# Turning x of eleven late chunks by DMA transposes on the SP queue instead of TensorE and ScalarE

## The chip, the cores and the metric

The kernel runs on one core of a Trainium2 chip. The metric is the device time of one execution in microseconds (us), the median of several runs. A core has four compute engines (TensorE, VectorE, ScalarE, GpSimd), a sequencer SP that here issues nearly all DMAs, and sixteen DMA engines that carry them. In the profile's lines PE is TensorE, PEld its weight loads, DVE VectorE, ACT ScalarE, POOL GpSimd; SPq is SP's sequencer.

## The reference

A gated linear attention with state runs over 768 positions for 4 batches and 8 heads of 48; its output, taken as x of 384 columns, goes through a gated MLP with a spatial mix.

```
state = alpha[t] * state + k[t] (outer) v[t];   y[t] = q[t] @ state        # 4 batches x 8 heads, head_dim 48
x = y as [4, 768, 384]
h = relu(x @ w_in);  u, v = halves of h (512 each)
v_n = (v - mean) / sqrt(var + 1e-6);  v_s = w_spatial @ v_n + b_spatial
out = (u * v_s) @ w_out
```

## The kernel before

The sequence is cut into 24 chunks of 128 positions, 6 per batch. Each chunk loads alpha, k, q, v (192 KB each, called ac, kc, qc, vc), computes y in PSUM and hands x to the second half, which needs it transposed as xT: the v matmuls of the same chunk, and the u matmuls of three chunks, read xT.

The order of all instructions is not written by hand. A small planner in the kernel gives each operation an estimated duration, plays all of them against each other with hints (NUDGE, PATIENCE), and emits each engine's program in the order that comes out. The planner's times are only used for that; on the chip the engines wait on semaphores. SP's program is part of the order, and in the traces below SP issues its DMAs in the order of its program.

```python
    def dma(key, us, emit, deps, prio, eng="SP", issue=0.99, lat=1.9):
        o = op(key + ("issue",), eng, issue, emit, deps, prio=prio)          # time of the issuing sequencer
        return op(key, "DMA", us, lambda _: None, [o], prio=prio, lat=lat)   # time of the DMA engines, then latency
...
        op(("xs", i), "ACT", 0.38, xs, ...)          # x_sb <- y: PSUM to SBUF, bf16
        def xt(_):                                   # three 128x128 transposes on TensorE, into y's PSUM bank
            for ks in range(KS):
                nc.tensor.transpose(xv[:, ks, :], st["x_sb"][:, ks, :], ident)
        op(("xt", i), "PE", 0.2, xt, got(("xs", i)), ...)
        op(("xe", i), ENGINES["xe"], None, xe, ...)  # xT <- PSUM, on ScalarE
...
        dma(("ac", i), LD, load("ac", alpha), io_users("ln", j), P, lat=LATE)      # kc, qc, vc likewise
...
        group(("v", b, tt), mms, 0.22, got(("xe", b * NCH + tt)) + made[("w_in", 1)], Q + tt, evac, ...)
```

Of the kernel before, what the change touches and what calls it, by code (L numbers as in the profile page):

```python
# [9 lines left out]
FP32 = mybir.dt.float32  # L10
# [41 lines left out]
class Clock:  # L52
# [34 lines left out]
NUDGE = {  # L87
    ("m", 9, 0): -0.15,
    ("vn", 0, 4): -0.3,
    ("qt", 22): -0.3,  # L90
    ("upd", 2): 0.3,
    ("v", 0, 5): 0.6,
    ("vbp", 0, 0): -0.6,
    ("z", 21): 1.5,
    ("ebc", 0): 0.15,
    ("ev", "q", 1, 1): 0.15,
    ("z", 19): -1.5,
    ("cast", "w_in", 0, 1): -0.15,
    ("vb", 21): -0.15,
    ("y", 19): -1.5,  # L100
    ("kc", 0): 1,
# [4 lines left out]
    ("y", 2): 0.15,  # L106
    ("xs", 22): -0.3,
    ("m", 20, 0): 0.6,
}
PAIRS = (0, 1, 2)  # L110
LATE = 3.5
ACT_STATS = ((2, 2), (0, 2))
PIECES = {
    "w_in": ((0, "vc", 1, 0.35), (0, "kc", 2, 0.15)),
    "w_sp": ((0, "vc", 4, 0.35), (0, "qc", 6, 0.25), (0, "qc", 6, 0.25)),
    "w_out": (0, "qc", 7, 0.25),
}

# [46 lines left out]
def kernel(  # L165
# [12 lines left out]
    nc = tc.nc  # L178

    B, H, S, D = q.shape  # L180
    C = 128
    NCH = S // C
    HP = H // 2
    DM = H * D
# [13 lines left out]
    WK = 3  # L198
# [3 lines left out]
    raws = ctx.enter_context(tc.tile_pool(name="raws", bufs=NRAW))  # L202
# [28 lines left out]
    def copy(eng, out, in_):  # L231
        if eng == "ACT":
            nc.scalar.copy(out=out, in_=in_)  # L233
        else:
            ENG[eng].tensor_copy(out=out, in_=in_)  # L235
# [79 lines left out]
    made = {}  # L315

    def op(key, *args, **kw):

        users = kw.pop("use", ())
        o = Op(*args, **kw)  # L320
        for s in users:
            s.users.append(o)
        ops.append(o)
        made[key] = o
        o.wait = PATIENCE.get(key[0], 0.0) + NUDGE.get(key, 0.0)
        return o

    def got(*keys):
        return [made.get(x) for x in keys]

    def dma(key, us, emit, deps, prio, eng="SP", issue=0.99, lat=1.9):
        o = op(key + ("issue",), eng, issue, emit, deps, prio=prio)
        return op(key, "DMA", us, lambda _: None, [o], prio=prio, lat=lat)
# [38 lines left out]
    def finish_x(i):  # L372

        b, c = divmod(i, NCH)
        t0 = c * C
        st = T[i]
        P = float(10 * i)

        def xs(eng):
            st["x_sb"] = work.tile([128, KS, 128], BF16, name="x_sb")  # L380
            copy(eng, st["x_sb"], st["y"].rearrange("p h d -> p (h d)").rearrange("p (k t) -> p k t", k=KS))

        op(("xs", i), "ACT", 0.38, xs, got(("y", i), ("xt", i - WK)), prio=P + 9, use=[st["sl_y"]])

        def xt(_):
            xv = st["xv"] = st["y"].rearrange("p h d -> p (h d)").bitcast(BF16)[:, 0:KS * 128].rearrange(
                "p (ks t) -> p ks t", ks=KS)
            for ks in range(KS):
                nc.tensor.transpose(xv[:, ks, :], st["x_sb"][:, ks, :], ident)  # L389

        op(("xt", i), "PE", 0.2, xt, got(("xs", i)), prio=P + 9, use=[st["sl_y"]], cols=384)

        def xe(eng):
            if c == 0:
                tiles(b)
            to, fr = bt[b]["xT"][:, :, t0:t0 + C], st["xv"]
            if i // 2 in PAIRS:
                to = to.rearrange("p k (t two) -> p k t two", two=2)
                fr = fr.rearrange("p k (two t) -> p k t two", two=2)
            copy(eng, to, fr)  # L400

        op(("xe", i), ENGINES["xe"], None, xe,
           got(("xt", i)) + [made.get(("all", b - 3))], prio=P + 9, use=[st["sl_y"]])

    def io_users(x, j, back=None):

        j = j - IO if back is None else j
        if x == "cum":
            return got(("cum", 2 * j), ("cum", 2 * j + 1), ("cump", j, 0), ("cump", j, 1))
        return got((x, 2 * j), (x, 2 * j + 1), (x + "p", j), (x + "p", j, 0), (x + "p", j, 1))  # L410
# [5 lines left out]
    def pair(j):  # L416
# [172 lines left out]
        for ci in range(2):  # L589
            i = 2 * j + ci  # L590
            T[i]["sl_y"] = Slot(rings["a"])

            def y(_, i=i, ci=ci):
                yt = T[i]["y"] = bank(pp_a, [128, H, D], FP32, name="y", tag="a")
                rows = halves(ci)
                n, tot = 0, 2 * H + (HP if i % NCH else 0)
                for h in range(H):
                    for par in range(2):
                        nc.tensor.matmul(  # L599
                            out=yt[:, h, :], lhsT=st[f"ptm{par}"][rows, h % 2, h // 2, :],  # L600
                            rhs=st["vb"][rows, par, h, :], start=(n == 0), stop=(n == tot - 1))
                        n += 1
                if i % NCH:
                    for hp in range(HP):
                        nc.tensor.matmul(
                            out=yt[:, 2 * hp:2 * hp + 2, :].rearrange("p s d -> p (s d)"),
                            lhsT=q_cols(slice(0, 128), hp, ci), rhs=sbd_bufs[(i - 1) % NB][:, hp, :],
                            start=False, stop=(n == tot - 1))
                        n += 1

            op(("y", i), "PE", 0.5, y,
               [made[("m", j, par, s)] for par in range(2) for s in range(2)]
               + got(("vbp", j, 0), ("vbp", j, 1)) + (got(("sb", i - 1)) if i % NCH else []), prio=P + 8 + ci, take=T[i]["sl_y"], cols=1024)
            finish_x(i)

    def first(i):
# [6 lines left out]
        def load(name, src):  # L623
            def emit(_):
                if i % 2 == 0:
                    T[i + 1][name + "2"] = st[name + "2"] = io_pool.tile([128, 2, H, D], FP32, name=name)
                t = st[name] = st[name + "2"][:, i % 2]
                nc.sync.dma_start(out=t, in_=src[b, :, t0:t0 + C, :].rearrange("h s d -> s h d"))
            return emit

        j = i // 2
        jo = j - NKP
        dma(("ac", i), LD, load("ac", alpha), io_users("ln", j), P, lat=LATE)
        dma(("kc", i), LD, load("kc", k), io_users("kt", j), P + 0.1, lat=LATE)
        dma(("qc", i), LD, load("qc", q), io_users("qt", j), P + 0.2, lat=LATE)
        dma(("vc", i), LD, load("vc", v), io_users("vb", j), P + 0.3, lat=LATE)

# [107 lines left out]
        def y(_):  # L745
# [16 lines left out]
        op(("y", i), "PE", 0.38 if c else 0.2, y, got(("m", i, 0), ("m", i, 1), ("vb", i), ("sb", i - 1) if c else None),  # L762
           prio=P + 8, take=st["sl_y"], cols=768)
        finish_x(i)


    bt = {}

    def tiles(b):
        d = bt[b] = {}  # L770
        d["xT"] = batch.tile([128, KS, S], BF16, name="xT")
        d["uT"] = batch.tile([128, NDS, S], BF16, name="uT")
        d["v_sb"] = batch.tile([128, NT, DH], BF16, name="v_sb", bufs=2)
        d["vn"] = batch.tile([128, NT, DH], BF16, name="vn", bufs=2)
        d["gT"] = batch.tile([128, NDS, S], BF16, name="gT", bufs=2)
        d["mvs"] = batch.tile([128, NT, 2], FP32, name="mvs")
        d["sums"] = batch.tile([128, 2, NT], FP32, name="sums")
        d["rstd"] = batch.tile([128, NT], FP32, name="rstd")
# [57 lines left out]
    def second_v(b, tt):  # L836
# [3 lines left out]
        t0 = tt - tt % 2  # L840
        on_act = (b, t0) in ACT_STATS

# [116 lines left out]
    kept = {}  # L959

    def out_tile(n):

        if n < 8 or n >= B * NT - 4:
            if n % 4 == 0:
                kept["t"] = raws.tile([128, 4 * DM], FP32, name="raw_w")
            return kept["t"][:, n % 4 * DM:(n % 4 + 1) * DM]
        if n < KEEP:
            return raws.tile([128, S], BF16, name="w_row", bufs=NROW).bitcast(FP32)
        return outp.tile([128, DM], FP32, name="o_sb")

    def second_o(b, tt):
# [14 lines left out]
        def evac(eng, ps):  # L986
            hold["o"] = out_tile(n)
            if n < B * NT - 1:
                copy(eng, hold["o"], ps[:, 0:DM])
                return  # L990
            half = DM // 2
            copy("ACT", hold["o"][:, 0:half], ps[:, 0:half])
            copy("DVE", hold["o"][:, half:DM], ps[:, half:DM])
# [61 lines left out]
    for b in range(B):  # L1055
        for c in range(NCH):
            i = b * NCH + c
            if i // 2 in PAIRS:
                if i % 2 == 0:
# [50 lines left out]
```

## Time and profile before

| | before |
|---|---|
| median of the device time | 154.93 us (154.78 to 155.08, 4 runs) |
| span of the profiled run | 153.4 us |
| TensorE's share of the chain that ended last | 86% |
| DMA occupancy, 80 to 100 us | 0.99 |
| granted TensorE clock | 0.999 |

### The profile page before, as it was taken

What the parts mean: (1) busy time and instruction counts of PE and PEld (TensorE: products, weight loads), DVE (VectorE), ACT (ScalarE), POOL (GpSimd) and SP (SyncE); (2) the same over time, 40 slices, a digit from 0 to 9 for tenths busy, and PEclk for the clock granted to TensorE, in tenths of its full rate; (3) what the DMA queues carried; (4) which work ended last, traced back from release to release, by engine and by line L of the source; (5) the groups of instructions that cost most, each with busy time, mean ns of one, the idle gap of its engine ahead of it and who ended that gap; (6) DMA issues with size and microseconds to landing.
All of it is one profiled execution on the core that took longest, in us unless ns stands there. A gap on an engine that the chain in (4) does not pass through costs nothing.

```text
span 153.4 us, 4488 instructions
## 1 busy us (share of the span) xinstructions
PE 146.1 (95%) x1720; PEld 91.7 (60%) x1720; DVE 119.9 (78%) x256; ACT 111.7 (73%) x270; POOL 87.5 (57%) x152
## 2 busy tenths in 40 slices
PE   6999999998999999999999999999999999999980
PEld 3466666766656656566666656666666666656540
DVE  7666689494879999897989999487979897756820
ACT  3496684797997878897976969899987657970150
POOL 6837558742369688762658867446587872005400
PEclk9999999999999999999999999999999999999999
DMA  4999999999999897999999999989970013400053
GB/s 121 265 313 291 314 245 264 257 294 178 242 247 287 174 197 154 215 184 199 190 193 196 199 174 201 214 155 214 372 281 4 4 38 115 153 6 0 0 205 105
DMA packets 93013, 28.60 MB, mean 186 GB/s; under 512 B 87872, under 2 KB 91456, under 8 KB 92992
## 3 DMA queue, kind: packets, MB, share of 16 engines
q1 hardware_dynamic: 92960, 28.32, 79.2%
q8 instruction: 13, 0.21, 0.6%
q14 instruction: 8, 0.07, 0.1%
q0 software_dynamic: 32, 0.00, 0.0%
HBM read 23.60 MB, written 4.72 MB: 185 GB/s over the span
## 4 chain that ended last, share of the span: by engine, by line
PE 86%; ACT 4%; DMA 3%; DVE 1%; issue 1%; POOL 1%; ACTq 0%
PE ps L801 49%; PE pt L698 6%; PE pt L728 3%; PE y L389 3%; DMA ac<-in_alpha_dram 3%; PE y L756 2%; PE cum L647 2%; PE ps L225 2%; PE tp L714 2%; PE ps L456 2%; PE y L599 2%; PE y L750 2%; PE ps L521 2%; PE ps L811 2%; PE y L225 2%
## 5 line engine op out<-in xcount | busy, mean ns | idle before, releaser
L801 PE MATMUL ps<-w_spT,vn 128*128 128x384 bf16 x192 | 36.1, 326 | 0.0
L954 POOL TENSOR_TENSOR gT<-vsb,uT 128x384 bf16<-128x384 f32 x28 | 25.6, 926 | 18.3 <-DVE vsb L941 17.7
L739 DVE TENSOR_TENSOR ptm<-pt,mask 128x512 bf16<-128x512 f32 x36 | 23.2, 682 | 5.1 <-PE pt L728 4.9
L671 POOL TENSOR_TENSOR kt<-kc,binv 128x384 bf16<-128x384 f32 x18 | 16.3, 914 | 17.9 <-ACT bc L666 7.1
L801 PEld LDWEIGHTS <-vn 128*128 128x128 bf16 x192 | 17.2, 97 | 9.7 <-issue 0.2
L801 PE MATMUL ps<-w_in,xT 128*128 128x512 bf16 x72 | 19.1, 380 | 0.1
L801 PE MATMUL ps<-xT,w_in 128*128 128x384 bf16 x96 | 18.4, 326 | 0.0
L801 PE MATMUL ps<-w_out_sb,gT 128*128 128x384 bf16 x96 | 18.2, 326 | 0.0
L941 DVE TENSOR_TENSOR vsb<-ps,bsp_bc 128x384 f32<-128x384 f32 x31 | 16.4, 548 | 2.2 <-PE ps L801 2.2
L863 DVE BATCH_NORM_STATS2 stats<-v_sb 128x6 f32<-128x512 bf16 x20 | 13.7, 685 | 5.0 <-ACT v_sb L239 4.8
L239 ACT ACTIVATE v_sb<-ps 128x512 bf16<-128x512 f32 x20 | 11.9, 597 | 6.0 <-PE ps L801 5.8
L360 POOL TENSOR_TENSOR state<-state,bc 128x192 f32<-128x192 f32 x17 | 8.7, 510 | 11.9 <-DVE state L353 7.3
L233 ACT CAST x_sb<-y 128x384 bf16<-128x384 f32 x24 | 11.5, 480 | 5.2 <-PE y L756 2.5
L235 POOL CAST sbd<-state 64x192 bf16<-64x192 f32 x40 | 13.8, 344 | 2.3 <-DVE state L360 0.6
L233 ACT COPY xT<-y 128x384 bf16<-128x384 bf16 x24 | 11.5, 479 | 2.0 <-PE y L389 1.4
L893 DVE TENSOR_SCALAR vn<-v_sb,mvs,rstd 128x512 bf16<-128x512 bf16 x24 | 12.2, 538 | 0.2
L801 PEld LDWEIGHTS <-gT 128*128 128x128 bf16 x96 | 8.9, 98 | 5.6
L801 PEld LDWEIGHTS <-w_in 128*128 128x128 bf16 x96 | 8.5, 97 | 5.1
L233 ACT COPY o_sb<-ps 128x384 f32<-128x384 f32 x9 | 4.3, 482 | 9.9 <-PE ps L801 9.9
L239 ACT ACTIVATE uT<-ps 128x384 bf16<-128x384 f32 x23 | 10.7, 487 | 0.4 <-PE ps L801 0.4
L681 DVE TENSOR_TENSOR qt<-qc,cum 128x384 bf16<-128x384 f32 x18 | 9.8, 548 | 0.8 <-ACT cum L676 0.6
L659 ACT ACTIVATE binv<-cum 128x384 bf16<-128x384 f32 x18 | 8.7, 492 | 2.2 <-POOL sbd L235 0.7
(129 smaller groups left out, 302.3 us busy)
## 6 DMA issues: line engine op xcount, KB each, us to landing
ac<-in_alpha_dram SPq DMA_DIRECT2D x18, 192.0 KB, 4.3
kc<-in_k_dram SPq DMA_DIRECT2D x18, 192.0 KB, 4.0
qc<-in_q_dram SPq DMA_DIRECT2D x18, 192.0 KB, 3.9
vc<-in_v_dram SPq DMA_DIRECT2D x18, 192.0 KB, 4.0
raw_w<-in_moe_w_spatial_dram SPq DMA_DIRECT2D x3, 768.0 KB, 5.6
out_dram<-raw_w SPq DMA_DIRECT2D x12, 192.0 KB, 2.8
out_dram<-o_sb SPq DMA_DIRECT2D x9, 192.0 KB, 1.9
raw_w<-in_moe_w_in_dram SPq DMA_DIRECT2D x2, 768.0 KB, 8.1
```

Source lines behind the costliest of these rows:

```text
L233: nc.scalar.copy(out=out, in_=in_)
L235: ENG[eng].tensor_copy(out=out, in_=in_)
L239: nc.scalar.activation(out=out, in_=in_, func=AF.Relu)
L671: ENG[eng].tensor_mul(out=kt[:, :, :, 0:D], in0=quad(st["kc"]), in1=st["binv"])
L681: nc.vector.tensor_mul(out=qt[:, :, :, 0:D], in0=quad(st["qc"]), in1=st["cv"])
L698: nc.tensor.transpose(t[:, HP * n + hp, :], src[:, hp, :, :], ident)
L739: nc.vector.tensor_tensor(out=st["ptm"][:, s], in0=st[f"pt{s}"], in1=mask4, op=ALU.mult)
L801: return lambda ps: nc.tensor.matmul(out=out(ps), lhsT=lhsT(), rhs=rhs(), start=start, stop=stop)
L863: nc.vector.bn_stats(out=stats, in_=d["v_sb"][:, tt, :])
L893: nc.vector.tensor_scalar(out=d["vn"][:, t, :], in0=d["v_sb"][:, t, :], scalar1=d["mvs"][:, t, 0:1], scalar2=d["rstd"][:, t:t + 1], op0=AL ...
L941: nc.vector.tensor_tensor(out=hold["vs"], in0=ps[:, 0:TH], in1=bsp_bc[:, th, :], op=ALU.add)
L954: ENG[eng].tensor_tensor(out=bt[b]["gT"][:, dsl, cols], in0=hold["vs"], in1=bt[b]["uT"][:, dsl, cols], op=ALU.mult)
```

## The change

The intent is to take 33 transposes off TensorE, which bounds the kernel, and 11 copies off ScalarE, and to let the DMA engines turn x. Some hints were re-tuned with it, and the statistics of two more chunks went from VectorE to ScalarE. The diff is cut, and short lines of NUDGE are joined.

```diff
 NUDGE = {
-    ("qt", 22): -0.3,  ("z", 19): -1.5,  ("cast", "w_in", 0, 1): -0.15,
+    ("v", 3, 4): 0.6,  ("cast", "w_in", 0, 2): 1,  ("cast", "w_in", 1, 0): -0.3,
+    ("z", 2): -0.3,  ("qtp", 2, 1): 1.5,  ("einvp", 0, 0): -1.5,
 ...
+BY_DMA = (12, 13, 15, 16, 17, 18, 19, 20, 21, 22, 23)
-ACT_STATS = ((2, 2), (0, 2))
+ACT_STATS = ((2, 2), (0, 2), (2, 4))
-    "w_sp": ((0, "vc", 4, 0.35), ...
+    "w_sp": ((0, "vc", 3, 0.35), ...
 ...
+        def turn(_):
+            if c == 0:
+                tiles(b)
+            nc.sync.dma_start(
+                out=bt[b]["xT"][:, :, t0:t0 + C], in_=st["x_sb"].rearrange("p k t -> p (k t)"), transpose=True)
+
+        if i in BY_DMA:
+            dma(("xe", i), 0.5, turn, got(("xs", i), ("all", b - 3)), P + 9, issue=1.0, lat=2.0)
+            return
 ...   # cut: xs waits for the transpose that last read its buffer; output tiles are kept by number
```

More of the change, by code (lines that the diff above doesn't have):

```diff
@@ L89 @@
     ("vn", 0, 4): -0.3,
-    ("qt", 22): -0.3,
     ("upd", 2): 0.3,
@@ L96 @@
     ("ev", "q", 1, 1): 0.15,
-    ("z", 19): -1.5,
-    ("cast", "w_in", 0, 1): -0.15,
     ("vb", 21): -0.15,
@@ L108 @@
     ("m", 20, 0): 0.6,
+    ("v", 3, 4): 0.6,
+    ("cast", "w_in", 0, 2): 1,
+    ("cast", "w_in", 1, 0): -0.3,
+    ("z", 2): -0.3,
+    ("qtp", 2, 1): 1.5,
+    ("einvp", 0, 0): -1.5,
 }
 PAIRS = (0, 1, 2)
+BY_DMA = (12, 13, 15, 16, 17, 18, 19, 20, 21, 22, 23)
 LATE = 3.5
-ACT_STATS = ((2, 2), (0, 2))
+ACT_STATS = ((2, 2), (0, 2), (2, 4))
 PIECES = {
     "w_in": ((0, "vc", 1, 0.35), (0, "kc", 2, 0.15)),
-    "w_sp": ((0, "vc", 4, 0.35), (0, "qc", 6, 0.25), (0, "qc", 6, 0.25)),
+    "w_sp": ((0, "vc", 3, 0.35), (0, "qc", 6, 0.25), (0, "qc", 6, 0.25)),
     "w_out": (0, "qc", 7, 0.25),
@@ L328, in got @@
     def got(*keys):
-        return [made.get(x) for x in keys]
+        return [made.get(x) for x in keys if x is not None]
     def dma(key, us, emit, deps, prio, eng="SP", issue=0.99, lat=1.9):
@@ L381, in xs @@
             copy(eng, st["x_sb"], st["y"].rearrange("p h d -> p (h d)").rearrange("p (k t) -> p k t", k=KS))
-        op(("xs", i), "ACT", 0.38, xs, got(("y", i), ("xt", i - WK)), prio=P + 9, use=[st["sl_y"]])
+        op(("xs", i), "ACT", 0.38, xs, got(("y", i), ("xt", i - WK), ("xe", i - WK) if i - WK in BY_DMA else None), prio=P + 9, use=[st["sl_y"]])
+        def turn(_):
[6 more added lines that the diff above has]
+            return
         def xt(_):
@@ L963, in out_tile @@
         if n < 8 or n >= B * NT - 4:
-            if n % 4 == 0:
-                kept["t"] = raws.tile([128, 4 * DM], FP32, name="raw_w")
-            return kept["t"][:, n % 4 * DM:(n % 4 + 1) * DM]
+            if n // 4 not in kept:
+                kept[n // 4] = raws.tile([128, 4 * DM], FP32, name="raw_w")
+            return kept[n // 4][:, n % 4 * DM:(n % 4 + 1) * DM]
         if n < KEEP:
```

## The prediction

> **What bounds the kernel now.** I read the page from the top down: busy shares, slices, chain; then single tiles, windows and timelines for the places the change touches.
>
> ```profile
> span 153.4 us, 4488 instructions
> PE 146.1 (95%) x1720; PEld 91.7 (60%) x1720; DVE 119.9 (78%) x256; ACT 111.7 (73%) x270; POOL 87.5 (57%) x152
> ...
> DMA  4999999999999897999999999989970013400053
> ...
> PE 86%; ACT 4%; DMA 3%; DVE 1%; issue 1%; POOL 1%; ACTq 0%
> ```
>
> The chain that ended last is TensorE for 86% of the span; no other engine holds more than 4%. The DMA row says something else: the sixteen DMA engines are full for three quarters of the span and nearly empty after about 113 us. So two things are tight at once until then, and one afterwards.
>
> A high PE busy figure alone proves little, because pipelined matmuls overlap. So I looked at pitches:
>
> ```profile
> 133.19 15.66 PE ps L801 x94
> ```
>
> This line of the chain is the tail: 94 matmuls in 15.66 us, 0.167 us each, though one lasts 326 ns in the table of groups. TensorE issues back to back there. I added up start-to-start pitches in the same way over 75 to 133 us, where the changed chunks lie, each shape at its own shortest pitch. What is left over as waiting, once the slow switches of the small 48-row matmuls are taken out, is about 2 us of 58. So TensorE's instruction stream sets the time, and a TensorE instruction removed there is worth its pitch, not its duration.[...]
>
> The work that the change takes out of TensorE and ScalarE:
>
> ```profile
> L389 PE MATMUL y<-ident,x_sb x72: 216/219/230, 16.7 to 133.0; 128*128 128x128 bf16 x72
> L233 ACT CAST x_sb<-y x24: 473/478/487, 16.1 to 132.1; 128x384 bf16<-128x384 f32 x24
> ...
> L233 ACT COPY xT<-y x24: 473/478/486, 17.0 to 133.2; 128x384 bf16<-128x384 bf16 x24
> ```
>
> and how such a triple sits in TensorE's stream, from a timeline of 0.8 us:
>
> ```profile
> 126.03 0.33 PE L389 MATMUL y<-ident,x_sb 128*128 128x128 bf16 x3
> 126.20 0.81 PE L801 MATMUL ps<-w_out_sb,gT 128*128 128x384 bf16 x4
> ```
>
> The next group starts 0.17 us after the triple began. That is what a triple costs: three pitches of about 56 ns, not 3 x 219 ns and not the 0.33 us of the line.
>
> The SP queue, which gets the new work, from the end of its timeline:
>
> ```profile
> 98.56 0.65 SPq L628 DMA_DIRECT2D vc<-in_v_dram  x1
> 99.27 0.97 SPq L628 DMA_DIRECT2D ac<-in_alpha_dram  x1
> 100.33 2.81 SPq L628 DMA_DIRECT2D kc<-in_k_dram  x2
> 103.23 1.41 SPq L628 DMA_DIRECT2D qc<-in_q_dram  x2
> 104.69 1.37 SPq L628 DMA_DIRECT2D vc<-in_v_dram  x1
> 106.11 4.43 SPq L1000 DMA_DIRECT2D out_dram<-raw_w  x8
> ```
>
> SP issues loads almost without a pause until 106 us, then the kept-back stores. An issue takes 0.4 to 3 us, mostly 0.7 to 1.2.
>
> **What the Trainium skill says.**
> - "Advanced Engine Details and Errata", section "X-Bar Transpose (TRN2)": transposing DMAs are as fast as regular ones. "DMA: Bandwidth & Descriptors", section "Latency and other measured facts", gives 261 GB/s for a measured one. No transposing DMA is in this trace. An estimate from that figure: 128 x 384 bf16 is 98,304 bytes, so 0.38 us of all sixteen engines. The trace moves 198 GB/s between 60 and 80 us at full DMA occupancy, a load of 192 KB thus taking about 1 us; half the bytes at that rate is 0.5 us. I take 0.4 to 0.5.
> - The same DMA page, "Anatomy of one DMA", says most of the fixed 2 us is the write receipt, and that DMA engines do not wait on semaphores: the issuing sequencer does. The trace agrees with the size: stores of 192 KB land 1.8 us after issue at the least, loads in the full stretch after 4.0 in the median. The second half means that SP stands still at each transpose until its x_sb is written, with the loads behind it.
> - "TensorE: Matmul & The Clock Gate", "Part 4: PE-mode transpose", gives 275 to 390 ns per 128 x 128 transpose. The trace has 219 ns of duration and 56 ns of pitch; the measurement decides.
>
> **The change, part by part.** Chunks 12, 13 and 15 to 23 lose the TensorE triple and the ScalarE copy from PSUM; x_sb is written as before and a DMA turns it.
>
> 1. TensorE: 11 triples x 0.168 us = 1.85 us, all on the path. This is the core of the gain: 1.2%.
> 2. ScalarE: 11 copies x 0.478 = 5.3 us less. The added entry of ACT_STATS moves the statistics of two chunks from VectorE to ScalarE: 2 x (0.63 Square + 0.19 accumulator read) and 2 more accumulator reads of 0.19, 2.0 us back. VectorE loses 2 x (0.69 + 0.18) = 1.7 and gains some 0.7 of tiny operations. Neither is the bound, so all of this is worth only what it removes of the roughly 2 us of TensorE waits.
> 3. PSUM: the y bank, one of two shared by cum, tp and y, is now free when x_sb is written, not when xT is. From the end of x_sb to the end of xT it is 0.9 to 1.6 us in the trace, so the bank comes free that much sooner. That helps against the same small rest of waits. For 2 and 3 together, with the re-tuned order, I put 0.4 us.
> 4. SP and DMA: in the trace x_sb of chunks 12, 13, 15, 16 and 17 is written between 75 and 104 us, while loads are still issued. Five to seven transposes x about 1 us of issue push the last load from 104.7 to some 111 us; the DMA engines get 7 x 0.5 = 3.5 us more. There is room: chunk 23's alpha is issued at 99.3 and read at 114.0, its v issued at 104.7 (4 us to landing) and read at 120.1, its q issued at 104.0 and read at 125.0. About 10 us of lead against 6 of delay: no cost.
> 5. Latency of xT: from the end of x_sb to xT ready are about 1.1 to 1.4 us now. By DMA it is 1 (issue) + 1.8 to 4 (landing) = 3 to 5 us. For chunks up to 22 TensorE has the matmuls of the batch before to do, and its order was re-planned for it. A mis-planned order costs up to 1 us in a few chunks; I put 0.2 in all.
> 6. The tail. Chunk 23 has nothing after it:
>
> ```profile
> 131.89 1.14 PE L801 MATMUL ps<-xT,w_in 128*128 128x384 bf16 x6
> 132.86 0.33 PE L389 MATMUL y<-ident,x_sb 128*128 128x128 bf16 x3
> 133.03 1.14 PE L801 MATMUL ps<-xT,w_in 128*128 128x384 bf16 x6
> 134.01 0.81 PE L801 MATMUL ps<-w_in,xT 128*128 128x512 bf16 x3
> 134.65 2.11 PE L801 MATMUL ps<-xT,w_in 128*128 128x384 bf16 x12
> 136.60 0.65 PE L801 MATMUL ps<-w_spT,vn 128*128 128x384 bf16 x3
> ```
>
> x_sb ends at 132.6 and the last v matmuls start at 134.0; by DMA they start 3 to 3.5 us after x_sb, not 1.4, so some 2 us later. What TensorE can do meanwhile: the twelve matmuls of the first u half (2.0 us), and the first four matmuls of four spatial groups, as many as there are PSUM banks (16 x 0.163 = 2.6 us): 4.6 us. What it has to bridge: about 3.2 us of transpose, and the 3.4 us from v to vn (134.65 to about 138.0 now) less the second u half of 2.0 us: 4.6. It just fits; I put a loss of 0.3 us.
>
> Sum: 154.9 - 1.85 - 0.4 + 0.2 + 0.3 = 153.15, say 153.1 us.
>
> **The rivals.**
> - *The DMA side becomes the bound.* For it: occupancy 0.99 between 80 and 100 us, SP without pauses, and a transposing DMA that may write in pieces smaller than the 192-byte packets of the loads. If it took 2 us of all engines and not 0.5, seven of them would delay the last loads by 14 us, past the 10 us of lead, and cum, kt and qt of the last chunks would be late: 156 to 160 us. Against it: only late chunks were chosen, and after 113 us the queue is idle.
> - *Latency shows.* Each v group waits for a DMA that the plan believed earlier, TensorE stalls 0.5 us in each of eleven chunks, or 2 us once at the tail, and the gain is eaten: 154.5 to 156. For it: a queue in order, behind loads, with 4.0 us to landing. Against: chunk 23 would hardly have been chosen had it stalled.
> - *Freed ScalarE and PSUM banks count for more.* The waits of TensorE in 75 to 133 us nearly vanish and the re-tuned start (first 40 us, where TensorE runs fillers and waits) gains a little: 151 to 151.8. Against: it needs nearly all of the 2 us.
>
> **Range and chances.** Only the third rival passes 2% (below 151.8 us), and it needs everything: 0.18. Slower than 158 needs a transpose several times dearer than estimated: 0.10. The rest is within 2%: 0.72. Range 151.4 to 155.5.
>
> **What would show it.** Right: 39 x_sb transposes left on TensorE (13 chunks), its busy time about 2 us lower in the table's pitch terms, ScalarE's total some 3 us lower, the last load issued near 111 us, landing of the transposes at 2 to 5 us. Wrong: waits of v's weight loads on a DMA of xT of more than 1 us in total, a gap in TensorE's stream after 130 us, la or kt waiting for loads of the last chunks, or a SP issue of a transpose much over 1 us.

## More of the kernel before

One stretch that the prediction did not show became the key: SP's timeline (start, duration, what was issued) around 75.6 us, the end of chunk 12's x_sb in this kernel:

```profile
75.79 0.94 SPq L628 DMA_DIRECT2D vc<-in_v_dram  x1
76.77 0.92 SPq L628 DMA_DIRECT2D ac<-in_alpha_dram  x1
...
84.13 0.99 SPq L628 DMA_DIRECT2D kc<-in_k_dram  x1
```

These are the loads of chunk 16's v, chunk 17's alpha and, 8 us later, chunk 18's k, counted off in order. Chunk 18's k is not read until 100.7 us, so whether SP gets to it at 76 or at 84 us makes no difference to this kernel.

## The result, and the profile after

The changed kernel takes 165.51 us (164.45 to 165.69, 4 runs) against 154.93: a ratio of 1.065 with an interval of 1.059 to 1.072. Ratios here are taken from the fast runs of both kernels in the same rounds, so not quite the ratio of the medians quoted. The prediction was 153.1 us, with 151.4 to 155.5 as its range.

The page of the changed kernel, the same rows as before and the row of the granted clock:

```profile
span 163.6 us, 4448 instructions
PE 146.2 (89%) x1677; PEld 91.9 (56%) x1693; DVE 118.9 (73%) x251; ACT 112.9 (69%) x273; POOL 86.2 (53%) x148
...
PEclk9999999999999999999955579999999999999999
DMA  5999999799989979989899999495856003440025
...
PE 79%; ACT 4%; DMA 4%; SPq 4%; DVE 3%; issue 2%; POOL 1%; DVEq 0%; ACTq 0%
```

SP's own issuing (SPq) is now in the chain that ended last, and in slices 21 to 23 the clock was granted at about half (0.7 in slice 24). TensorE's timeline around there (start, duration, line, operation, what ended the idle time before it):

```profile
80.21 0.40 PE L712 MATMUL pt<-ident,qt 128*128 128x128 bf16 x4
89.89 0.61 PE L815 MATMUL ps<-w_in,xT 128*128 128x512 bf16 x1 [9.28 <-DMA xT<-x_sb]
90.72 0.63 PE L815 MATMUL ps<-w_in,xT 128*128 128x512 bf16 x1 [0.22 <-issue]
```

TensorE started nothing from 80.4 to 89.9 us and was idle for 9.28 us, for one xT, that of chunk 12. In four windows (us, then busy time of each engine, the granted clock, the DMA share and GB/s), before, during and after the stall:

```profile
75.00:80.40 5.40, 5.40 (x76) 3.65 (x73) 5.20 (x11) 4.53 (x14) 2.70 (x6) 1.00 0.96 189
80.40:89.90 9.50, 0.22 (x5) 0.05 (x3) 0.92 (x2) 0.63 (x2) 0.91 (x1) 0.61 0.99 196
89.90:96.20 6.30, 6.08 (x45) 3.25 (x47) 3.45 (x7) 2.46 (x6) 2.96 (x5) 0.50 0.98 195
96.20:102.00 5.80, 5.75 (x58) 3.36 (x56) 3.76 (x8) 4.75 (x12) 3.45 (x5) 1.00 1.07 211
```

The other compute engines all but stop with TensorE (0.6 to 0.9 us busy of 9.5); the DMA engines do not. For 6.3 us after the stall TensorE runs at half clock. Start to start, the stall is 9.4 us longer than a pitch, and 6.3 us at half clock cost an estimated 3.1 us more (half of 6.3). Together with the 1.85 us that the prediction reckoned for the matmuls taken off TensorE: 154.9 + 9.4 + 3.1 - 1.85 = 165.55, and 165.51 was measured. So close a sum is no proof of its terms; that one stall and its wake are the whole loss is shown by the last run below.

Why was this xT so late? ScalarE wrote chunk 12's x_sb between 75.29 and 75.76 us. ScalarE's line and SP's timeline:

```profile
75.29 0.48 ACT L237 CAST x_sb<-y 128x384 bf16<-128x384 f32 x1 [0.17 <-PE y L770]
```
```profile
74.80 1.73 SPq L642 DMA_DIRECT2D ac<-in_alpha_dram  x2
...
85.84 0.69 SPq L642 DMA_DIRECT2D kc<-in_k_dram  x1
86.63 1.79 SPq L392 DMA_TRANSPOSE xT<-x_sb  x1
88.53 0.52 SPq L642 DMA_DIRECT2D qc<-in_q_dram  x1
```

SP never waits for x_sb here. It issues loads the whole time, from chunk 16's alpha up to chunk 18's k, because they stand ahead of the transpose in its program. The transpose goes out 10.9 us after its data was ready and lands 3.2 us later, at 89.84 us; TensorE goes on at 89.89.

The transposes themselves behaved as estimated (the lines of the tile xT; durations are minimum, median and maximum in ns, landing counted from the issue):

```profile
L237 ACT COPY xT<-y x13: 460/478/485, 16.7 to 98.2; 128x384 bf16<-128x384 bf16 x13
L392 SPq DMA_TRANSPOSE xT<-x_sb x11: 1185/1193/1795, 86.6 to 141.4; - x11
...
DMA to landing us min/median/max: 2.3/2.5/4.1
```

The page's queue 1 took 77.8% of 163.6 us where it took 79.2% of 153.4: 127.3 against 121.5 us of all engines, so an estimated 0.53 us for each of eleven transposes. The transposes' own packets of 256 bytes, which the kernel before has none of, took 5.17 us of all engines, 0.47 us each.

The planner's own numbers explain the order. They are a plan, read out while the kernel was built, and not a measurement: in it SP is done with chunk 18's k at 73.3 us and with the transpose next, at 74.3; x_sb is done at 73.1. On the chip x_sb was done 2.7 us later than planned (75.8), but SP was done with that k load 13 us later than planned (86.5). Most of the lag is the length of SP's issues: the plan has 53.5 us for the 55 from chunk 6's alpha to that load, the chip took 64.6, one after the other. For loads, planned far ahead of their use, this lag costs nothing, which is why the kernel before runs well with it. A transpose has no such lead and takes over the full lag.

### The profile page after: what moved, and what is told of

It is laid out like the page before. It is cut to its first block, busy times and chain, and to the rows that moved or that the text cites. A ratio compares the mean times of both kernels' runs of the same rounds, so it can differ in the third digit from the quotient of the medians.

```text
span 163.6 us, 4448 instructions
## 1 busy us (share of the span) xinstructions
PE 146.2 (89%) x1677; PEld 91.9 (56%) x1693; DVE 118.9 (73%) x251; ACT 112.9 (69%) x273; POOL 86.2 (53%) x148
## 3 DMA queue, kind: packets, MB, share of 16 engines
q1 hardware_dynamic: 97536, 29.40, 77.8%
## 4 chain that ended last, share of the span: by engine, by line
PE 79%; ACT 4%; DMA 4%; SPq 4%; DVE 3%; issue 2%; POOL 1%; DVEq 0%; ACTq 0%
PE ps L815 46%; PE pt L712 4%; SPq L642 4%; PE pt L742 3%; PE y L770 2%; DMA ac<-in_alpha_dram 2%; PE cum L661 2%; PE tp L728 2%; DMA xT<-x_sb 2%; PE y L229 2%; PE y L613 2%; PE y L764 2%; PE ps L535 2%; PE ps L229 1%; PE ps L470 1%
## 5 line engine op out<-in xcount | busy, mean ns | idle before, releaser
L815 PE MATMUL ps<-w_spT,vn 128*128 128x384 bf16 x192 | 37.1, 335 | 0.0
L815 PE MATMUL ps<-w_in,xT 128*128 128x512 bf16 x56 | 17.0, 388 | 10.8 <-DMA xT<-x_sb 9.3
L815 PEld LDWEIGHTS <-vn 128*128 128x128 bf16 x192 | 17.7, 100 | 11.0 <-issue 1.4
L243 ACT ACTIVATE v_sb<-ps 128x512 bf16<-128x512 f32 x18 | 10.8, 600 | 11.9 <-PE ps L815 11.4
L877 DVE BATCH_NORM_STATS2 stats<-v_sb 128x6 f32<-128x512 bf16 x18 | 12.3, 685 | 3.9 <-ACT v_sb L243 3.9
L815 PEld LDWEIGHTS <-xT 128*128 128x128 bf16 x72 | 6.2, 98 | 15.7 <-DMA xT<-x_sb 9.4
L359 DVE TENSOR_TENSOR state<-tp,state 128x192 f32<-128x192 f32 x16 | 5.6, 349 | 12.7 <-PE tp L728 11.9
L243 ACT ACTIVATE uT<-ps 128x384 bf16<-128x384 f32 x25 | 11.7, 491 | 0.3 <-PE ps L815 0.2
```

The lines of the kernel that those rows point to most:

```text
L243: nc.scalar.activation(out=out, in_=in_, func=AF.Relu)
L815: return lambda ps: nc.tensor.matmul(out=out(ps), lhsT=lhsT(), rhs=rhs(), start=start, stop=stop)
L877: nc.vector.bn_stats(out=stats, in_=d["v_sb"][:, tt, :])
```

## The experiments

I call this explanation theory A: the transposes are late by their place in SP's program. Rivals were B (the transposing DMA, or loads and transposes together, are too much for SP and the DMA engines) and C (the re-tuned order of the other engines costs the time). All kernels gave correct results. All times are medians of 4 executions, one of them the profiled one (6 for the last two). The diffs are cut to what matters, and the comments in them are this document's; where the list BY_DMA changes, a line that makes the xT tile at its first use is left out. That the other four engines have the same instructions in the same order, where it is said, was compared in the traces.

### Other places in SP's program: a first try

The planner's decisions stay; loads from a given chunk on are held back at emission until the named transpose is out. On the other four engines the instructions are the same, in the same order.

```diff
+BEFORE_LOADS = {12: 17, 13: 18, 15: 21, 16: 21, 17: 23}   # transpose of chunk 12 ahead of chunk 17's loads, ...
```

> Only SP's order differs from the changed kernel: each early transpose stands ahead of the loads that SP reaches at about that time (chunk 12's ahead of chunk 17's loads, not behind those of 18). TensorE, ScalarE, VectorE and GpSimd have the same instructions in the same order. Theory A (the transpose of chunk 12 was late because it stood behind loads that SP had not yet got to): the 9.5 us stall of TensorE and the halved clock after it vanish, 152.5 to 154.5 us. Rival B (the transposing DMA itself, or the load on the DMA engines, is too slow): the stall stays in some form, 160 us or more. Rival C (the re-tuned order of the other engines costs the time): 163 us or more.

Measured: 168.54 us, ratio 1.087. The stall of 9.5 us did go: chunk 12's transpose was issued at 80.3 us and the stall there is 3.1 us. But a new one of 5.9 us arose at chunk 17, whose x_sb was ready at 105.4 us:

```profile
109.65 0.69 SPq L654 DMA_DIRECT2D qc<-in_q_dram  x1
110.43 1.09 SPq L654 DMA_DIRECT2D vc<-in_v_dram  x1
111.61 1.39 SPq L393 DMA_TRANSPOSE xT<-x_sb  x1
```

It had been put behind all loads of chunks 21 and 22. With each of the two stalls came 6.8 us of halved clock. The miss refutes C in its simple form (the stall moved though the order of the engines was the same), but not B: my places were still too late, and the result alone cannot tell that from an overload.

### Issued from ScalarE

```diff
-            nc.sync.dma_start(
+            nc.scalar.dma_start(
                 out=bt[b]["xT"][:, :, t0:t0 + C], in_=..., transpose=True)
```

> Only the queue differs from the changed kernel: the eleven transposes are issued by ScalarE, at the place in its order where the plan put them, just behind their x_sb. Theory A: no loads stand ahead of them, so the stall vanishes; ScalarE pays some 1.2 us of issue each, 13 us in all of an engine busy 69%, so small waits elsewhere: 153 to 157 us. Rival B (transposes slow in the DMA engines beside the loads): x_sb to landing of over 8 us and a stall of about 9 us again, 160 us or more.

Measured: 163.30 us, ratio 1.054, outside what A expected. Yet the stall is gone: chunk 12's transpose was issued at 76.04 us, 0.03 us after x_sb, landed at 81.31, and TensorE's longest gap after 40 us is 1.6 us. The clock stayed at 1.000. In its place are a dozen gaps of 0.5 to 1.6 us. From 75 to 133 us ScalarE spends 1.2 us on each issue instead of computing, and TensorE, VectorE and GpSimd are all busy for less of the time (line of the windows view, then the landing times of its transposes):

```profile
75.00:133.00 58.00, 50.55 (x572) 31.37 (x571) 42.76 (x91) 40.10 (x104) 33.55 (x54) 1.00 0.85 169
```
```profile
DMA to landing us min/median/max: 2.3/4.0/5.8
```

TensorE was busy 50.55 of these 58 us; the kernel before had it 57.56 of the 57.9 us from 75.1 to 133.0. So moving the issue to a busy compute engine trades one stall for many waits. That the issues on ScalarE cause these waits fits the trace, but was not separated from the longer landing (4.0 us in the median, 2.5 on SP).

### Only chunks 18 to 23

```diff
-BY_DMA = (12, 13, 15, 16, 17, 18, 19, 20, 21, 22, 23)
+BY_DMA = (18, 19, 20, 21, 22, 23)
```

> Only chunks 18 to 23 are turned by DMA; their x_sb is written at 109 us or later, when SP has issued all loads. Theory A: no stall, and a gain of six triples, 6 x 0.17 = 1.0 us, against a cost at the tail of at most 0.5: 153.5 to 155 us. Rival D (latency of every transpose costs TensorE something, here at the tail above all): 155.5 to 158 us.

Measured: 168.88 us, one slow run of the four included (the fast three: 168.66); the ratio of its fast runs is 1.087. A's number was wrong, for a reason of A's own kind. The profiled execution was the slow one (170.1 us, against 167.4 to 169.1 of the others), so its order of events is used and its times are only a guide. Chunk 18's x_sb ends at 111.4 us in it, and SP does this:

```profile
110.19 5.03 SPq L1014 DMA_DIRECT2D out_dram<-raw_w  x8
115.32 1.39 SPq L1014 DMA_DIRECT2D out_dram<-w_row  x3
...
117.31 2.59 SPq L392 DMA_TRANSPOSE xT<-x_sb  x2
```

The loads were done, but the kept-back stores stood ahead. TensorE waited 5.9 us for chunk 18's xT and 3.1 us for chunk 23's. The planner also orders everything anew when the list changes, so this run does not isolate one cause.

### The re-tuning alone

```diff
-BY_DMA = (12, 13, 15, 16, 17, 18, 19, 20, 21, 22, 23)
+BY_DMA = ()
```

> The re-tuning of the change (order hints, the third pair of statistics on ScalarE, the earlier weight piece) without any DMA transpose. Theory A: the re-tuning is worth less than 1 us either way, 154 to 156 us. Rival C (the re-tuned order is itself what costs): 160 us or more.

Measured: 165.41 us, ratio 1.068, as slow as the changed kernel and as rival C expected. The trace says that it is another loss. There is no stall near 80 us. With no DMA transposes in it the planner orders everything anew, and puts the last chunks so late that TensorE has nothing beside them (its timeline near the end):

```profile
136.91 0.40 PE L712 MATMUL pt<-ident,kt 128*128 128x128 bf16 x4 [0.71 <-POOL kt L685]
...
139.03 0.40 PE L742 MATMUL pt<-kqT 48*128 48x128 bf16 x8 [1.10 <-ACT kqT L237]
...
142.91 1.46 PE L815 MATMUL ps<-w_in,xT 128*128 128x512 bf16 x3 [0.57 <-ACT xT L237]
```

Chunk 23's x_sb ends at 141.8 us, against 132.6 in the kernel before. The hints belong to one plan and mean little in another, so this run could not decide about C. The next one could.

### The DMA transposes with the hints of before

NUDGE, ACT_STATS and the weight pieces are those of the kernel before; BY_DMA and its code are the change's.

> Only the DMA transposes of the change, with the order hints, the statistics and the weight pieces of the kernel before. The planned SP order again has chunk 12's transpose behind 18's k load. Theory A: the same stall of 8 to 11 us at chunk 12, 162 to 168 us. If the re-tuned hints were the cause: 153 to 157 us.

Measured: 164.29 us, ratio 1.061. TensorE has the same stall at chunk 12, 7.5 us long, with half clock for 6.8 us. x_sb ends at 75.55 us; SP again comes from chunk 18's k load:

```profile
83.57 0.72 SPq L639 DMA_DIRECT2D kc<-in_k_dram  x1
84.38 1.58 SPq L389 DMA_TRANSPOSE xT<-x_sb  x1
```

So the re-tuned hints are not needed for the loss.

### Keeping TensorE warm through the stall

```diff
+        if (b, tt) == (2, 0):      # chunk 12's v group: 54 filler matmuls 128x384 ahead of its first matmul
+            mms[0] = warm
```

> The changed kernel with 54 filler matmuls (8.8 us of TensorE) placed just before chunk 12's first v matmul, where TensorE otherwise stands still for 9.5 us; nothing else moves. Theory A's account of the loss is 9.4 us of stall and 3.1 us because the clock stays halved for 6.3 us after it: with the fillers the clock stays whole, the stall itself stays, so 165.5 - 3.1 = 162.4, between 161.5 and 163.5 us. If the halved clock costs nothing: 165 us or more.

Measured: 163.90 us (ratio 1.058), 1.6 us better than the changed kernel where 3.1 was expected. The stall is filled and the clock is whole:

```profile
80.40:89.90 9.50, 9.34 (x61) 5.52 (x60) 1.09 (x2) 0.80 (x2) 0.91 (x1) 1.00 1.05 203
89.90:96.20 6.30, 5.14 (x62) 3.16 (x60) 3.70 (x8) 3.91 (x8) 3.88 (x6) 1.00 0.86 171
```

The clock's share is seen at the next x_sb: chunk 14's ends at 93.8 us against 96.8 in the changed kernel, 3.0 us earlier, as expected. But chunk 15's is only 1.7 us earlier. What is missing lies in the second window. TensorE, now faster, reaches chunk 13's v group at 94.1 us and waits 1.3 us, until 95.4, for a transpose that had been hidden behind the half clock. 3.1 - 1.3 = 1.8 us, close to the 1.6 measured. So the halved clock is a real part of the loss, 3.0 us, but some 1.3 us of it covered the next late transpose.

### Chunk 12's transpose alone moved ahead

The two lines are the orders of SP's program, the planner's and the new one; the first stands in no code.

```diff
-# SP: ac16 ac17 kc16 qc16 vc16 kc17 qc17 vc17 ac18 ac19 vc18 kc18 T12 qc18 kc19 qc19 vc19 T13 ...
+# SP: ac16 T12 ac17 kc16 qc16 vc16 kc17 qc17 vc17 ac18 ac19 vc18 kc18 qc18 kc19 qc19 vc19 T13 ...
```

> The changed kernel with chunk 12's transpose alone moved ahead in SP's order, from behind chunk 18's k to behind chunk 16's alpha, 10 loads earlier; the other engines' order is the same. Theory A: its lateness (10.9 us from x_sb to issue) falls to under 2 us, but chunk 13's transpose still stands 14 loads later, is issued near 91 to 93 us and stops TensorE there for 5 to 9 us: 159 to 166 us with the stall at chunk 13. A rival by which the first transposing DMA has a cost of its own once: the stall stays at chunk 12.

Measured: 165.27 us, ratio 1.066. Chunk 12's transpose went out at 75.87 us, 0.03 us after x_sb, and its v group started without a stall. The stall stands one chunk later, as expected:

```profile
84.65 0.39 PE L713 MATMUL pt<-ident,qt 128*128 128x128 bf16 x4
93.87 1.46 PE L816 MATMUL ps<-w_in,xT 128*128 128x512 bf16 x3 [8.83 <-DMA xT<-x_sb]
```

So the first transposing DMA showed no cost of its own. Chunk 13's transpose was issued at 90.6 us, 9.9 us after its x_sb. In the changed kernel a like lateness (10.9 us) cost nothing, because TensorE had already lost its time at chunk 12. After its stall SP has caught up: from chunk 15 on the changed kernel issues every transpose within 0.12 us of its x_sb. Whichever transpose came first paid for that, in both runs.

### All transposes placed by hand

```diff
+SP_ORDER = """ac16 T12 kc16 qc16 vc16 ac17 T13 kc17 qc17 vc17 ac18 kc18 qc18 vc18 ac19 kc19 qc19 T15 vc19
+ac20 kc20 qc20 vc20 ac21 kc21 qc21 vc21 T16 ac22 T17 kc22 qc22 vc22 ac23 kc23 T18 qc23 T19 vc23""".split()
```

> The changed kernel with all of SP's order from chunk 16's loads on written out by hand, each of the transposes of chunks 12 to 19 placed at the load that SP reached, in the run without transposes, when its x_sb was done; the other engines' order is the same as in the changed kernel. Theory A: every transpose is issued within 2 us of its x_sb, stalls of TensorE on xT below 3 us in all, no halved clock: 153.5 to 158 us. Rival B (loads and transposes together are more than SP and the DMA engines can carry): a stall on loads or on xT of 4 us or more remains, 160 us or more.

Measured: 162.42 us, ratio 1.048: a miss of A's number and within the time that B expected, though no single wait on xT reached B's 4 us. Chunks 12 and 13 had no stall. But now TensorE ran ahead, chunks 17 and 18 had their x_sb up to 6.5 us earlier than in the kernel before, and the transposes of 16, 17 and 18 were again behind loads, issued 5.1, 4.6 and 7.8 us after x_sb; the clock was halved for 3.4 us. All waits of weight loads on xT (total us, times, longest us):

```profile
PEld L816 <- DMA xT<-x_sb: 8.3, 5, 3.2
```

Loads were no problem: chunk 22's and 23's landed some 10 us before they were read. That is the point that spoke for A against B, and gave the next placement.

### Placed again, with the stores behind

```diff
-... qc19 T15 vc19 ac20 kc20 qc20 vc20 ac21 kc21 qc21 vc21 T16 ac22 T17 kc22 qc22 vc22 ac23 kc23 T18 qc23 T19 vc23
+... qc19 T15 vc19 ac20 kc20 qc20 T16 vc20 ac21 T17 kc21 qc21 T18 vc21 ac22 kc22 T19 qc22 vc22 ac23 kc23 qc23 vc23
+S0 ... S11      # the twelve stores of finished outputs behind all loads
```

> As sp_place, with the transposes of chunks 16 to 19 each 2 to 5 loads earlier (in sp_place they were still issued 5.1, 4.6, 7.8 and 3.2 us after their x_sb) and the kept-back stores behind all loads; the other engines' order is still the changed kernel's. The last loads had about 10 us of lead in sp_place. Theory A: all transposes are issued within 2.5 us of x_sb, TensorE waits for xT less than 2 us in all, the clock stays whole: 153.0 to 156.5 us. Rival B (SP and DMA cannot carry loads and transposes together): stalls of 3 us or more stay, on xT or on loads of chunks 21 to 23, 158 us or more.

Measured: 154.97 us, ratio 0.997 with an interval of 0.993 to 1.002. Against the changed kernel, only SP's order differs (transposes, loads and stores), and the whole loss of 10.5 us is gone. This refutes B, and C too, as the re-tuned order of the other engines is still there. The clock is 0.999. What is left of waits on xT:

```profile
PEld L816 <- DMA xT<-x_sb: 1.9, 2, 1.4
```

### One more step

```diff
-... kc19 qc19 T15 vc19 ... vc21 ac22 kc22 T19 qc22 ...
+... kc19 T15 qc19 vc19 ... vc21 T19 ac22 kc22 qc22 ...
```

> As sp_place2, with chunk 15's transpose one load and chunk 19's two loads earlier. In sp_place2 TensorE still waited 0.7 us for chunk 15's xT and 1.5 us for chunk 19's, though both were issued within 1.3 us of x_sb: they landed 2.9 and 4.8 us after it, behind loads already given to the DMA engines. Theory A: with fewer loads in front they land earlier, the waits fall below 1 us together, and some 1 to 1.5 us of the removed TensorE work shows: 153.3 to 154.5 us. Rival: the loads pushed back by SP's standing still become the wait instead (chunks 20 and 21's v landed only 0.1 us before they were read in sp_place2): 154.7 us or more.

Measured: 154.12 us (153.73 to 154.72, 6 runs) against 154.85 of the kernel before in the same rounds: ratio 0.9956, interval 0.9942 to 0.9970. It beats both kernels, the one before by only 0.4%, which is clear of the noise. The wait view and SP's timeline at chunk 12 (x_sb ends at 75.78 us):

```profile
PEld L816 <- DMA xT<-x_sb: 0.2, 1, 0.2
```
```profile
75.80 1.28 SPq L393 DMA_TRANSPOSE xT<-x_sb  x1
77.20 0.93 SPq L643 DMA_DIRECT2D kc<-in_k_dram  x1
```

Chunk 19's transpose, issued as promptly as in the run before (0.03 us after x_sb against 0.25), landed 2.3 us after x_sb against 5.0 (the expectation's 2.9 and 4.8 us were counted from the issue). That fits the two loads fewer in front of it.

With this run the changed kernel's loss can be placed, since the other four engines have the same instructions in the same order. Chunk 13's x_sb ends at 80.62 us in the changed kernel and at 80.63 here, but chunk 14's at 96.80 against 84.56:

```profile
96.32 0.48 ACT L237 CAST x_sb<-y 128x384 bf16<-128x384 f32 x1 [1.65 <-PE y L770]
```
```profile
84.08 0.48 ACT L238 CAST x_sb<-y 128x384 bf16<-128x384 f32 x1
```

Chunk 23's is still 12.0 us later, and so is the end of the span (163.6 against 151.6 us). All of the loss lies between chunks 13 and 14, in the stall and the half-clock stretch behind it.

| kernel | what differs | us | ratio to before |
|---|---|---|---|
| the change | | 165.51 | 1.065 |
| sp_order | SP's order, first try | 168.54 | 1.087 |
| act_raw | issued by ScalarE | 163.30 | 1.054 |
| late_only | chunks 18 to 23, re-planned | 168.88 (one of 4 slow) | 1.087 |
| tune_only | no DMA transposes, re-planned | 165.41 | 1.068 |
| orig_hints | hints of before, re-planned | 164.29 | 1.061 |
| warm_fill | fillers in the stall | 163.90 | 1.058 |
| t12_alone | SP's order, one transpose | 165.27 | 1.066 |
| sp_place | SP's order by hand | 162.42 | 1.048 |
| sp_place2 | SP's order by hand, again | 154.97 | 0.997 |
| sp_place3 | SP's order by hand, last | 154.12 | 0.996 |

## Why the prediction was wrong

- **Step 5, latency of xT, failed.** It gave "1 (issue) + 1.8 to 4 (landing) = 3 to 5 us" from the end of x_sb and put 0.2 us in all. It assumed that SP issues the transpose when x_sb is done. For chunk 12 the terms measured were 10.9 us of standing behind loads, then 3.2 us from issue to landing: 14.1 us, of which TensorE's other work covered 4.7. The prediction had even written that SP "stands still at each transpose until its x_sb is written, with the loads behind it". For chunks 12 and 13 it was the other way round: the transpose stood behind the loads. The sign that it named for being wrong came true: weight loads waited 9.4 us on xT, against the 1 us that it allowed. (Its "about 1.1 to 1.4 us now" is 0.9 to 1.6 us in the trace, as its own step 3 has it; this changes nothing.)
- **The clock after a stall was missing from the sum.** It had no term for it: an estimated 3.1 us by the trace's windows, 3.0 us at the next x_sb with the fillers, 1.6 us net of them.
- **Step 1 held in kind and is only partly seen in the time.** The 33 transposes are gone from TensorE. Of the 1.85 us for them 0.7 us shows in the best order's median. By the spans from the first to the last instruction it is 1.1 us (medians 152.0 against 153.1), so some 0.4 us of it is lost outside the spans. Where the rest went is not settled; the re-planned order of TensorE differs from that of before everywhere.
- **Steps 2 and 3**, small gains from ScalarE and PSUM, were not tested by themselves. But ScalarE was not relieved: its busy time was to fall by some 3 us and rose from 111.7 to 112.9 us, because the re-planned order gave it other work in place of the eleven copies, above all 3 more kqT copies (3.0 us) and 4 more vb casts (2.0 us).
- **Step 4's sizes held, its conclusion did not.** The transpose costs SP 1.19 us and the DMA engines some 0.5 us, as estimated; the last load was issued at 113.4 us in the changed kernel, and TensorE's long stall was for xT and not for a load. But "no cost" looked only at what transposes do to loads.
- **Step 6, the tail, held.** In the changed kernel chunk 23's transpose landed 2.4 us after x_sb, and after 120 us no TensorE instruction starts more than 0.45 us after the one before.
- **The rivals.** "Latency shows" named the right place, a queue in order behind loads, but sized it at 0.5 us a chunk or 2 us once; and it argued against itself that chunk 23 "would hardly have been chosen had it stalled". That a change was tuned says nothing about the stall at chunk 12. "The DMA side becomes the bound" is refuted in the form given: loads and transposes fit once ordered, at 154.1 us. "Freed ScalarE and PSUM banks count for more" is not seen: no run came under 153.7 us, and ScalarE was not freed.

## What to carry to other kernels

A queue that issued in order without a pause ran 13 us late here against the plan that ordered it, and work with a long lead hid this. Before putting latency-bound work into such a queue, find in the trace what the queue is issuing at the moment the new work becomes ready, and place it there; then look again, because removing one stall moves all later moments. A stall can cost more than its length when the TensorE clock drops with it: here 3.0 us on top of 9.4, 1.6 us of it net.

## What the Trainium skill lacked or had wrong

- "DMA: Bandwidth & Descriptors", "Anatomy of one DMA" (headed for DMAs from GpSimd; those here are SP's), says that the issuing sequencer waits and the DMA engines do not; the trace agrees: from chunk 15 on SP issued each transpose of the changed kernel within 0.12 us of x_sb. It does not warn of the reverse case, a ready transfer behind others in the sequencer's program, which cost 10.9 us here.
- The same page, "Latency and other measured facts", has a bandwidth of transposing DMAs but no time from issue to landing of a small one from SBUF to SBUF. Measured for 128 x 384 bf16: 1.19 us of SP (median), at least 2.3 us from issue to landing, 2.5 in the median from SP, 4.0 from ScalarE's queue; 0.47 to 0.53 us of all engines, against an estimate of 0.38 by the page's 261 GB/s. The trace has 4,576 more packets for eleven transposes, 416 each, of which 384 carry 256 bytes.
- "TensorE: Matmul & The Clock Gate", "What's actually happening", lists half clock after an idle window of about 3.4 us. The runs agree in part: every stall of 3.1 to 9.4 us brought a half-clock stretch of 3.4 to 13.7 us, and gaps of up to 1.6 us in the ScalarE run brought none. But in the changed kernel the clock was halved at 82.5 us, 1.9 us after TensorE's last matmul had ended. And in the run of the re-tuning alone no gap between matmuls after 40 us exceeds 1.4 us, yet with TensorE busy 2.67 of 5.1 us (135.0 to 140.1 us) the clock was halved for 6.8 us. The same page, "A second HAM failure mode: psum-queue depth-cycling", does tell of frequent short idling after which the clock swings between half and full; it has no measure of how much idling is needed.
